# A fused attention and two-MLP kernel: every step that opens a PSUM bank takes the one of all eight that has been free longest

## The chip, the cores and the metric

One core of a Trainium2 chip. The metric is the device time of one execution in microseconds (us), lower is better. Before the change: 908.99 us, the median of 3 runs (908.58 to 909.68).

## The reference, cut to what matters

Linear attention over 4 batches of 8 heads with 576 tokens and 64 features, then two MLPs of 512 to 2048 to 512 on the 2304 tokens, with different activations; everything in float32.

```python
def phi(x):
    proj = np.einsum('bhsd,df->bhsf', x, w_phi)
    proj = proj - np.max(np.abs(proj), axis=-1, keepdims=True)
    return np.concatenate([np.exp(proj), np.exp(-proj)], axis=-1)
q_p, k_p = phi(q), phi(k)
kv = np.einsum('bhsf,bhsd->bhfd', k_p, v)
z = np.sum(k_p, axis=2)
num = np.einsum('bhsf,bhfd->bhsd', q_p, kv)
den = np.einsum('bhsf,bhf->bhs', q_p, z)[..., None] + 1e-06
x = num / den
...
h = x @ w_in                                   # MLP 1
x = np.where(h > 0.0, h, np.exp(np.minimum(h, 0.0)) - 1.0) @ w_out
...
h = x @ w_in                                   # MLP 2
x = (h * np.clip(h + 3.0, 0.0, 6.0) / 6.0) @ w_out
```

## The kernel before, in words

**Attention** runs in eight units (`unit`, L350) of one head pair and two batches. For a unit the steps are, with the names that the tables use:

- `PJ` (`proj`, L416): projections of k and q by `w_phi`, with 64 rows of the array each, in groups k0, k1, q0, q1 and x8 (the ninth block of both). A group opens two PSUM banks, one per head (h = 0, 1).
- `MX`, `SB` (`peak` L429, `shift` L437) on VectorE: the largest magnitude of a row, and the projection less it, out of PSUM into SBUF. The second of them frees the bank.
- `EX` on ScalarE (two exponentials), then `KV` (`kv`, L471): the sums over the tokens, 64 columns of the array wide, in two accumulator banks per unit; its x8 part uses 64 rows and 64 columns. `ST` on ScalarE copies the accumulators out.
- `QT` (`q_tr` L495, `q_tr8` L501): PE transposes of the shifted q, whole array; `QE` on ScalarE takes exponentials out of that bank.
- `NM` (`num`, L524): numerator and denominator, 64 columns wide, in three parts (ch = 0, 1, 2); `RT`, `RB` on VectorE divide; `XT` (`x_tr`, L552) transposes the quotient on PE, whole array; `XC` (`x_out`, L559) on ScalarE copies it to the MLP's input `x`.

**The MLPs** split a float32 value into two fp32r parts, form Strassen-like sums of blocks of x and w_in on VectorE, ScalarE and GpSimdE, and run 16 groups g of feature tiles each way: `hid` (L810, "P": six matmuls of 512 columns into an "h" bank), `hid4` (L824, "H": the block of the last 256 tokens), `join` (L842), the activation, `gate_lo` (L865, the last reader of an h bank, on VectorE), `outp` (L868, "O": the second matmul, into a "y" bank) and `sums` (L889, which adds the y bank to x and frees it). The first x blocks are used while the last attention unit still runs. The order of P, H and O on PE is written out in a list; PE's MLP steps follow it.

**What sets the order.** All of it is a list of `Step`s with engine, estimated duration, predecessors, and `Token`s that it takes from rings of buffers. `in_order` (L148) plays them against a model: per engine it takes, among the steps that could start within 0.3 us of the earliest, the one with the least rank. Ranks come from the tables `BIAS` (attention steps, by name, with other values in the first and last unit) and `SHIFT` (MLP steps), and `ON_POOL` names the steps that go to GpSimdE. `TURN` is the model's charge where PE goes from one shape of the array to another. The semaphores come from the data and buffers, so a step waits on the chip for whatever it needs, whenever that is.

**PSUM before.** The eight banks have fixed purposes. In attention four banks "p" take the projections in turn, two ("a0", "a1") the KV accumulators, two ("t") everything else (QT, NM, XT). In the MLPs the h steps take p0, p1, p2, p3, t1 in turn, the y steps a0, a1, t0 (`mlp_bank`, L711). A step that opens a bank waits for the readers of the one whose turn it is:

```python
BANKS = {"p": PB, "a0": 1, "a1": 1, "t": TB}
def bank(ring, shape=(128, 512)):
    i = count[ring] = count.get(ring, -1) + 1
    tag = ring if ring[-1].isdigit() else f"{ring}{i % BANKS[ring]}"
    return psum.tile(list(shape), F32, tag=tag, name="ps_" + tag)
...
HB, YB = ["p0", "p1", "p2", "p3", "t1"], ["a0", "a1", "t0"]
```

Of the kernel before, what the change touches and what calls it, by code (L numbers as in the profile page):

```python
# [8 lines left out]
F32 = mybir.dt.float32  # L9
# [13 lines left out]
PB, TB = 4, 2  # L23
# [94 lines left out]
}  # L118
ON_POOL = """
a01S20 a01S31 a10S10 a10S21 a10S30 a11S10 a11S11 l00S40 l00S41 l01A121 l01S41 l04x0 l04x1 l04x2  # L120
l10A220 l10S10 l10S21 l10S31 l11A110 l11S11 l11S41 l14x0 l14x1 l14x2
""".split()


# [23 lines left out]
def in_order(steps, rings):  # L148
# [30 lines left out]
    known = {}  # L179
# [1105 lines left out]
```

## Time and profile before

| | before |
|---|---|
| median of 3 runs | 908.99 us |
| the profiled execution's own time | 909.42 us |
| its span, first to last instruction | 907.6 us |
| PE (matmuls) busy | 894.1 us, 99% |
| VectorE busy | 662.1 us, 73% |
| ScalarE busy | 568.5 us, 63% |
| GpSimdE busy | 401.0 us, 44% |
| granted TensorE clock | 1.000 |
| matmul instructions in the trace | 6800 |

Attention takes the first 150 us or so, and the first MLP matmuls stand among its last ones; the first H step starts at 165.4 us; the second MLP begins near 526 us. After PE's last matmul some 3.9 us are left for the last sum and the last store. A float32 matmul outside the MLPs appears twice in the trace, so that 16 calls of `KV` are 32 matmuls of a row.

The busy share of PE counts each matmul from its start to a modelled end, and matmuls overlap. Idle time in a row stands behind the first instruction after it, with the instruction that is thought to have ended it.

### The profile page before, as it was taken

Reading aid. Unit: us, or ns where it says so; the run is one execution under the profiler, and the core shown is the slowest. Engines: PE = TensorE matmul, PEld = TensorE weight load, DVE = VectorE, ACT = ScalarE, POOL = GpSimd, SP = SyncE. Lnnn points to the kernel's source line nnn. Section 1 sums busy time; section 2 is a strip of 40 time slices with the busy share of each in tenths; the row PEclk is TensorE's granted clock in tenths of the full one; section 3 lists DMA queues with packets and bytes.
Section 4 is the critical chain, followed back from the end, with each engine's and each line's share of the span. In section 5 each row is a group of like instructions: output and inputs, shape, how many; then the busy total and the mean of one; then the engine's idle time right before and its main releaser. Section 6 shows DMA issues by size and latency. Waiting matters only on the chain.

```text
span 907.6 us, 17628 instructions
## 1 busy us (share of the span) xinstructions
PE 894.1 (99%) x6800; PEld 760.3 (84%) x6800; DVE 662.1 (73%) x1200; ACT 568.5 (63%) x1207; POOL 401.0 (44%) x574
## 2 busy tenths in 40 slices
PE   8999999999999999999999999999999999999998
PEld 7888888888888888888888878888888888888886
DVE  6888886856677676767677897577767666766655
ACT  6787777877665656666566777765545454546331
POOL 1447623244535353535343675665544444444200
PEclk9999999999999999999999999999999999999999
DMA  8544410001211111111111101112111111110013
GB/s 242 167 122 116 132 61 16 1 12 37 71 34 59 35 59 35 57 36 43 52 35 62 32 12 36 59 59 70 47 47 47 47 48 47 36 57 24 1 70 139
DMA packets 42675, 53.62 MB, mean 59 GB/s; under 512 B 21344, under 2 KB 21728, under 8 KB 42592
## 3 DMA queue, kind: packets, MB, share of 16 engines
q1 hardware_dynamic: 42448, 52.44, 18.7%
q8 instruction: 53, 0.87, 0.4%
q14 instruction: 30, 0.25, 0.1%
q10 hardware_dynamic: 144, 0.07, 0.0%
HBM read 47.78 MB, written 4.72 MB: 58 GB/s over the span
## 4 chain that ended last, share of the span: by engine, by line
PE 95%; DVE 2%; ACT 2%; issue 0%; DMA 0%; DVEq 0%
PE ps_a L884 29%; PE ps_p L818 27%; PE ps_t L884 14%; PE ps_t L818 6%; PE ps_t L534 4%; PE ps_p L422 4%; PE ps_a L484 4%; PE ps_p L832 3%; PE ps_t L498 2%; PE ps_t L832 1%; PE ps_t L556 1%; DVE mx L432 0%; ACT x L560 0%; ACT e L511 0%; DMA wphi<-in_w_phi_dram 0%
## 5 line engine op out<-in xcount | busy, mean ns | idle before, releaser
L818 PE MATMUL ps_p<-x_S,w_in 128*128 128x512 f32 x630 | 157.3, 390 | 0.0
L901 DVE TENSOR_TENSOR x<-ps_a,x 128x512 f32<-128x512 f32 (+1 forms) x178 | 116.6, 657 | 46.3 <-PE ps_a L884 44.1
L818 PEld LDWEIGHTS ps_p<-x_S,w_in 128*128 128x128 f32 x630 | 117.9, 188 | 24.4
L776 POOL TENSOR_TENSOR w_in<-w_bi,w_in 128x256 fp32r<-128x256 f32 x128 | 95.7, 766 | 73.9 <-ACT w_in L772 73.4
L818 PE MATMUL ps_p<-x_A,w_in 128*128 128x512 f32 x468 | 117.3, 390 | 1.4 <-DVE ga L866 1.4
L818 PEld LDWEIGHTS ps_p<-x_A,w_in 128*128 128x128 f32 x468 | 87.0, 188 | 19.2 <-DVE ga L866 1.6
L743 POOL TENSOR_SCALAR w_a<-w_a 128x256 f32<-128x256 f32 x128 | 53.5, 419 | 100.6 <-ACT w_a L738 97.1
L759 POOL TENSOR_TENSOR w_bi<-w_bi,w_a 128x256 int32<-128x256 int32 x64 | 49.2, 770 | 107.6 <-DVE w_a L755 107.6
L901 DVE TENSOR_TENSOR x<-ps_t,x 128x512 f32<-128x512 f32 (+1 forms) x89 | 59.0, 663 | 40.0 <-PE ps_t L884 39.0
L884 PE MATMUL ps_a<-w_out,gb 128*128 128x512 f32 (+1 forms) x342 | 82.7, 385 | 0.0
L884 PE MATMUL ps_a<-gb,w_out 128*128 128x512 f32 (+1 forms) x384 | 82.0, 355 | 0.6 <-DVE x L901 0.6
L785 POOL TENSOR_TENSOR w_out<-w_bo,w_out 128x256 fp32r<-128x256 f32 x64 | 48.0, 749 | 66.3 <-ACT w_out L781 65.6
L759 POOL TENSOR_TENSOR w_bo<-w_bo,w_a 128x256 int32<-128x256 int32 x64 | 48.6, 761 | 62.0 <-DVE w_a L755 62.0
L884 PEld LDWEIGHTS ps_a<-gb,w_out 128*128 128x128 f32 x384 | 65.2, 189 | 11.8 <-DVE x L901 0.8
L884 PEld LDWEIGHTS ps_a<-w_out,gb 128*128 128x128 f32 x342 | 63.5, 188 | 12.9
L884 PE MATMUL ps_a<-ga,w_out 128*128 128x512 f32 x258 | 64.0, 390 | 0.0
L859 DVE SCALAR_TENSOR_TENSOR ps_p<-ma,ps_p 128x512 f32<-128x512 f32 x66 | 45.8, 694 | 24.6 <-ACT ma L855 12.3
L884 PE MATMUL ps_a<-w_out,ga 128*128 128x512 f32 x240 | 58.5, 390 | 0.0
L840 ACT COPY mb<-ps_p 128x512 f32<-128x512 f32 x54 | 31.8, 588 | 41.4 <-PE ps_p L818 41.3
L432 DVE TENSOR_REDUCE mx<-ps_p 128x4 f32<-128x512 f32 (+1 forms) x80 | 49.7, 629 | 10.1 <-PE ps_p L422 10.1
L884 PEld LDWEIGHTS ps_a<-ga,w_out 128*128 128x128 f32 x258 | 47.8, 188 | 9.5
L738 ACT ACTIVATE w_a<-w 128x256 f32<-128x256 f32 x128 | 54.5, 426 | 0.5 <-POOL w_bi L759 0.3
(113 smaller groups left out, 1895.4 us busy)
## 6 DMA issues: line engine op xcount, KB each, us to landing
w<-in_moe_w_in_dram SPq DMA_DIRECT2D x64, 256.0 KB, 2.6
w<-in_moe_w_out_dram SPq DMA_DIRECT2D x64, 256.0 KB, 2.6
vb<-in_v_dram SPq DMA_DIRECT2D x16, 288.0 KB, 4.5
out_dram<-x SPq DMA_DIRECT2D x17, 256.0 KB, 2.0
raw_k<-in_k_dram SPq DMA_DIRECT2D x7, 576.0 KB, 4.7
raw_q<-in_q_dram SPq DMA_DIRECT2D x7, 576.0 KB, 4.0
raw_k<-in_k_dram SPq DMA_DIRECT2D x1, 320.0 KB, 4.1
raw_q<-in_q_dram SPq DMA_DIRECT2D x1, 320.0 KB, 4.5
```

The lines of the kernel that those rows point to most:

```text
L422: nc.tensor.matmul(out=ps[h][:, i * NF:(i + 1) * NF], lhsT=raw[s_][p, r * 128:(r + 1) * 128], rhs=wphi[p], start=True, stop=True,)
L432: V.tensor_reduce(out=mx[:, :n], in_=P[j, h], axis=AX.X, op=ALU.max, apply_absolute_value=True)
L484: nc.tensor.matmul(out=acc[bb][f0:f0 + 64, h, half], lhsT=kp[p, i, half, f0:f0 + 64], rhs=vb[u % 2][p, r, h], start=(done.count(bb) == 1 a ...
L738: nc.scalar.activation(out=st["a"], in_=s.bitcast(F32).rearrange("p (n t) -> p n t", t=2)[:, :, 1], func=AF.Abs)
L743: nc.gpsimd.tensor_scalar(out=st["a"], in0=st["a"], scalar1=W_MOST, scalar2=W_LEAST, op0=ALU.min, op1=ALU.max)
L759: nc.gpsimd.tensor_tensor(out=b_, in0=b_, in1=st["a"].bitcast(I32), op=ALU.add)
L776: nc.gpsimd.tensor_tensor(out=t[:, 1], in0=F[key], in1=t[:, 0].bitcast(F32), op=ALU.subtract)
L785: nc.gpsimd.tensor_tensor(out=t[:, 1], in0=F.pop((m, w, 1, c)), in1=t[:, 0].bitcast(F32), op=ALU.subtract)
L818: nc.tensor.matmul(out=PS[ps_], lhsT=t[:, a_, kk], rhs=X[pr, op][x_][kk], start=(opens and i == 0), stop=(i == 5), skip_group_check=True,)
L859: V.scalar_tensor_tensor(out=PS[ps_], in0=MAIN[key], scalar=s, in1=PS[ps_], op0=o0, op1=o1)
L884: nc.tensor.matmul(out=o, lhsT=a_, rhs=b_, start=(fi + j == 0), stop=(fi == 1 and j == 2), skip_group_check=half is not None,)
L901: V.tensor_tensor(out=part, in0=ps, in1=part, op=ALU.add)
```

## The change

`Token` gets a field `bank`. `in_order` keeps which token holds each of the eight banks; a step that opens a bank is possible once so many banks are free, and gets the one that has been free longest by the model. Rings still cap how many tokens of a kind are in use: p 6 instead of 4, t 4 instead of 2, a0 and a1 2 each instead of 1, h 5 and y 3 as before. So a projection group can open banks while five others are full, three groups in a row can be projected into six banks, and an h step can take a bank that last held a y tile. The four filling matmuls `WM` of the first unit now take a t token. The opening conditions "y" and "n" no longer wait for the users of the attention banks. `BIAS`, `SHIFT` and `ON_POOL` have new values throughout, so the order of the steps on all engines is new, in attention above all; the written list of P, H and O is the same.

```diff
-PB, TB = 4, 2
+PB, TB = 6, 4
...
-    "EX": 1217.6, "EXk00": -706.6, "EXk00@7": -744.6, "EXk01": 1256.6, "EXk01@0": 1292.5,
+    "EX": 813.1, "EXk00": -417.0, "EXk00@0": -376.4, "EXk00@7": -446.2, "EXk01": 875.0,
...
-        self.ring, self.users = ring, []
+        self.ring, self.users, self.bank = ring, [], None
...
+IN_BANKS = ("p", "a0", "a1", "t", "h", "y")
...
+    held = [None] * 8
+
+    def bank_free():
+        t = []
+        for k in held:
+            ends = [x.end for x in k.users] if k else []
+            t.append(None if None in ends else max([0.0] + [x.end + x.lag for x in k.users]) if k else 0.0)
+        return t
...
+        n = sum(k.ring in IN_BANKS for k in s.takes)
+        if n:
+            some = sorted(x for x in free_at if x is not None)
+            if len(some) < n:
+                return None
+            t = max(t, some[n - 1])
         return t
...
+            if k.ring in IN_BANKS:
+                t = bank_free()
+                k.bank = min((x, i) for i, x in enumerate(t) if x is not None)[1]
+                held[k.bank] = k
...
-    BANKS = {"p": PB, "a0": 1, "a1": 1, "t": TB}
-    rings = dict(BANKS)
-    count = {}
-
-    def bank(ring, shape=(128, 512)):
-        i = count[ring] = count.get(ring, -1) + 1
-        tag = ring if ring[-1].isdigit() else f"{ring}{i % BANKS[ring]}"
-        return psum.tile(list(shape), F32, tag=tag, name="ps_" + tag)
+    rings = {"p": PB, "a0": 2, "a1": 2, "t": TB}
+
+    def bank(i, kind, shape=(128, 512)):
+        return psum.tile(list(shape), F32, tag=f"b{i}", name=f"ps_{kind}{i}")
...
-            ps = [bank("p") for _ in range(2)]
+            ps = [bank(Tk["p", j, h].bank, "p") for h in range(2)]
...
-                add("WM", "PE", FILL * 0.218, fill, behind=[S_[pj]])
+                Tk["wm"] = take("t")
+                add("WM", "PE", FILL * 0.218, fill, behind=[S_[pj]], takes=[Tk["wm"]], uses=[Tk["wm"]])
...
-        "y": step("NONE", 0.0, y_open, after=y_users, rank=BEGIN),
-        "n": step("NONE", 0.0, y_open, after=n_users, rank=BEGIN),
+        "y": step("NONE", 0.0, y_open, rank=BEGIN),
+        "n": step("NONE", 0.0, y_open, rank=BEGIN),
...
-    def mlp_bank(ring):
-        i = nxt[ring] = nxt.get(ring, -1) + 1
-        tag = (HB if ring == "h" else YB)[i % rings[ring]]
-        return psum.tile([128, 512], F32, tag=tag, name="ps_" + tag)
-
...
-            PS[ps_] = mlp_bank("h")
+            PS[ps_] = bank(ptok[ps_].bank, "h")
```

Three places in the new order. In the rows a PSUM tile is named by its bank before the change (p0 to p3, a0, a1, t0, t1) and by its kind and bank number after it (p, a, t, n, h, y with 0 to 7); the number behind it counts tiles.

**Place 1: PE, where one attention unit passes into the next.** Before, one of six equal passages: XT, the transpose of x8, two NM parts, the next unit's first two KV steps, XT.

```order
L556 MATMUL ps_t1_2284<-ident_66,nr_2273 128x128 x3
L504 MATMUL ps_t0_2290<-ident_66,sh8_1879 128x128 x2
L534 MATMUL ps_t1_2302<-st_2182,e_2172 64x65 x4
...
L534 MATMUL ps_t0_2334<-st_2182,e_2232 64x65 x4
...
L484 MATMUL ps_a0_2369<-vb0_105,kp_2331 64x65 x16
L484 MATMUL ps_a1_2370<-vb0_105,kp_2364 64x65 x16
L556 MATMUL ps_t1_2420<-ident_66,nr_2367 128x128 x3
```

With the change, a passage between two units:

```order
L518 MATMUL ps_t0_2116<-ident_66,shq_1702 128x128 x4
L524 MATMUL ps_t4_2126<-ident_66,sh8_1357 128x128 x2
L518 MATMUL ps_t3_2133<-ident_66,shq_1933 128x128 x4
L518 MATMUL ps_t6_2140<-ident_66,shq_1886 128x128 x4
L554 MATMUL ps_n1_2153<-st_1754,e_1849 64x65 x4
...
L554 MATMUL ps_n0_2189<-st_1754,e_2130 64x65 x4
...
L504 MATMUL ps_a4_2229<-vb0_105,kp_2181 64x65 x16
```

Before, the first NM opens t1, which the XT two rows above it filled; now the transposes stand together, in four different banks, and the NM parts open two others.

**Place 2: PE, second MLP, first feature group.** The last terms of the first pair of token blocks (P3 and P4), H, and the first two terms of the second pair. Before:

```order
L818 MATMUL ps_p2_6771<-x_S4_0_2948,w_in_6689 128x512 x6
L818 MATMUL ps_t1_6853<-x_A22_0_114,w_in_6820 128x512 x6
L832 MATMUL ps_p1_6885<-x_b4_2949,w_in_6687 128x256 x6
L832 MATMUL ps_p1_6885<-x_b4_2949,w_in_6689 128x256 x6
L818 MATMUL ps_p2_6950<-x_A11_1_3135,w_in_6654 128x512 x6
L818 MATMUL ps_p3_6963<-x_A12_1_3136,w_in_6672 128x512 x6
```

With the change:

```order
L833 MATMUL ps_h3_6770<-x_S4_0_2830,w_in_6692 128x512 x6
L833 MATMUL ps_h6_6852<-x_A22_0_114,w_in_6756 128x512 x6
L847 MATMUL ps_h7_6878<-x_b4_2831,w_in_6690 128x256 x6
L847 MATMUL ps_h7_6878<-x_b4_2831,w_in_6692 128x256 x6
L833 MATMUL ps_h0_6944<-x_A11_1_3141,w_in_6654 128x512 x6
L833 MATMUL ps_h2_6956<-x_A12_1_3142,w_in_6656 128x512 x6
```

The order is the same; the last two steps open banks 0 and 2, which held y tiles of the first MLP, instead of p2, which P3 filled four rows above, and p3.

**Place 3: PE, the end of attention, up to the first H.** Before:

```order
L534 MATMUL ps_t0_3063<-st_2897,e_3004 64x65 x4
L818 MATMUL ps_p0_2952<-x_S4_0_2948,w_in_828 128x512 x6
L818 MATMUL ps_p2_2984<-x_A22_0_114,w_in_968 128x512 x6
L556 MATMUL ps_t1_3115<-ident_66,nr_3060 128x128 x3
L556 MATMUL ps_t0_3122<-ident_66,nr_3103 128x128 x3
L832 MATMUL ps_t1_3146<-x_b4_2949,w_in_398 128x256 x6
```

With the change:

```order
L833 MATMUL ps_h1_2832<-x_S4_0_2830,w_in_903 128x512 x6
L833 MATMUL ps_h2_2931<-x_A22_0_114,w_in_987 128x512 x6
L576 MATMUL ps_t0_3035<-ident_66,nr_3022 128x128 x3
L518 MATMUL ps_t5_3040<-ident_66,shq_2811 128x128 x4
L524 MATMUL ps_t4_3046<-ident_66,sh8_2518 128x128 x2
L554 MATMUL ps_n3_3057<-st_2808,e_2898 64x65 x4
...
L554 MATMUL ps_n7_3087<-st_2808,e_2926 64x65 x4
L576 MATMUL ps_t0_3119<-ident_66,nr_3115 128x128 x3
L576 MATMUL ps_t5_3130<-ident_66,nr_3126 128x128 x3
L847 MATMUL ps_h4_3151<-x_b4_2831,w_in_625 128x256 x6
```

Before, two MLP terms stand between the last NM and the last two XT; now those terms come first, and the last QT, both NM parts and the last two XT follow one another directly.

## Rows read from the trace of the kernel before

**Rows 1.** The page: span and PE's busy time.

```profile
span 907.6 us, 17628 instructions
PE 894.1 (99%) x6800; PEld 760.3 (84%) x6800; DVE 662.1 (73%) x1200; ACT 568.5 (63%) x1207; POOL 401.0 (44%) x574
```

**Rows 2.** Stretches: length, then busy us (instructions) per engine, clock, DMA share, GB/s.

```profile
62.39:80.44 18.05, 17.70 (x403) 15.90 (x404) 16.18 (x34) 14.99 (x37) 11.18 (x14) 1.00 0.48 133
165.37:520.00 354.63, 354.63 (x1731) 300.50 (x1732) 255.78 (x458) 239.46 (x495) 165.19 (x238) 1.00 0.13 42
520.00:550.00 30.00, 27.95 (x144) 23.61 (x143) 28.71 (x43) 21.10 (x43) 21.02 (x21) 1.00 0.03 9
```

**Rows 3.** PE's waits, whole span: waiting line, releaser, us in total, times, longest.

```profile
PE ps_t L534 <- ACT x L560: 2.1, 6, 0.4
PE ps_p L818 <- DVE ga L866: 1.4, 1, 1.4
PE ps_p L422 <- PE ps_a L404: 0.9, 1, 0.9
PE ps_a L484 <- issue: 0.9, 1, 0.9
PE ps_t L534 <- ACT e L511: 0.7, 1, 0.7
PE ps_a L884 <- DVE x L901: 0.6, 1, 0.6
PE ps_t L534 <- ACT st L493: 0.5, 1, 0.5
PE ps_t L832 <- ACT x L560: 0.2, 1, 0.2
PE ps_p L422 <- DVE shk L446: 0.2, 1, 0.2
```

**Rows 4.** ScalarE's timeline: the copy of a quotient, and a pair of exponentials.

```profile
61.86 0.48 ACT L560 COPY x<-ps_t 128x384 f32<-128x384 f32 x1 [0.77 <-PE ps_t L556]
77.45 1.09 ACT L511 ACTIVATE e<-ps_t 128x512 f32<-128x512 f32 x2
```

**Rows 5.** The chain of waits in one attention unit: start, us, what.

```profile
62.39 3.02 PE ps_t L534 x96
65.41 1.87 PE ps_a L484 x64
70.36 1.08 PE ps_a L484 x32
71.92 0.44 PE ps_t L498 x4
73.44 0.59 PE ps_t L498 x4
74.03 0.65 PE ps_p L422 x8
75.26 1.56 PE ps_t L534 x48
77.41 1.98 PE ps_p L422 x32
```

**Rows 6.** PE's timeline: two steps that waited.

```profile
9.32 1.16 PE L422 MATMUL ps_p<-wphi,raw_k 64*128 64x128 f32 x16 [0.95 <-PE ps_a L404]
544.25 3.02 PE L818 MATMUL ps_p<-x_A,w_in 128*128 128x512 f32 x12 [1.43 <-DVE ga L866]
```

**Rows 7.** VectorE's timeline: two last readers of a bank, and the division of one NM part.

```profile
8.54 0.68 DVE L446 TENSOR_TENSOR shk<-ps_p,mx 128x512 f32<-128x512 f32 x1
65.46 0.17 DVE L542 TENSOR_SCALAR dn<-ps_t 128x6 f32<-128x6 f32 x1 [0.42 <-PE ps_t L534]
65.88 0.56 DVE L547 TENSOR_TENSOR nr<-ps_t,dn 128x384 f32<-128x384 f32 x1
543.50 0.69 DVE L866 TENSOR_TENSOR ga<-ps_p,ga 128x512 fp32r<-128x512 f32 x1
```

More of the change, by code (lines that the diff above doesn't have):

```diff
@@ L65 @@
 SHIFT = {
[52 rows of a table removed]
[53 rows of a table added]
 }
 ON_POOL = """
-a01S20 a01S31 a10S10 a10S21 a10S30 a11S10 a11S11 l00S40 l00S41 l01A121 l01S41 l04x0 l04x1 l04x2
-l10A220 l10S10 l10S21 l10S31 l11A110 l11S11 l11S41 l14x0 l14x1 l14x2
+a01S11 a01S41 a10S10 a10S21 a10S30 a11S10 a11S20 a11S40 l00S40 l00S41 l01S10 l01S21 l01S40 l04x0
+l04x2 l10A220 l10S10 l10S21 l11A121 l11A220 l11S21 l11S31 l14x1 l14x3
 """.split()
@@ L176, in soonest @@
                 t = max(t, x.end + x.lag)
+        n = sum(k.ring in IN_BANKS for k in s.takes)
[4 more added lines that the diff above has]
+            t = max(t, some[n - 1])
         return t
-    known = {}
     while len(out) < len(steps):
         best = None
+        free_at = bank_free()
         for e, some in ready.items():
@@ L328, in attention_then_two_mlps @@
     wphi = apool.tile([128, NF], F32, name="wphi")
-    warm = bank("t")
+    warm = bank(7, "w")
     for _ in range(WARM):
@@ L401, in fill @@
         def fill():
-            ps = bank("a1")
+            ps = bank(Tk["wm"].bank, "w")
             for _ in range(FILL):
@@ L474, in kv @@
                 for bb in range(2):
-                    acc[bb] = bank(f"a{bb}", (128, 2, 2, D + 1))
+                    acc[bb] = bank(Tk["acc", bb].bank, "a", (128, 2, 2, D + 1))
             rs = [r for s_, r in ITEMS[j] if s_ == "k"]
@@ L495, in q_tr @@
         def q_tr(h, c):
-            ps = bank("t")
+            ps = bank(Tk["q", h, c].bank, "t")
             for i in range(4):
@@ L501, in q_tr8 @@
         def q_tr8():
-            ps = bank("t")
+            ps = bank(Tk["q", 8].bank, "t")
             for h in range(2):
@@ L524, in num @@
         def num(ch):
-            ps = bank("t", (128, 3, 2, D + 1))
+            ps = bank(Tk["n", ch].bank, "n", (128, 3, 2, D + 1))
             for i in range(3):
@@ L552, in x_tr @@
         def x_tr(ch):
-            ps = bank("t")
+            ps = bank(Tk["x", ch].bank, "t")
             nr = NR.pop(ch).rearrange("p i h d -> p i (h d)")
@@ L571, in unit @@
             tp = {(j, h): take("p") for j in js for h in range(2)}
+            Tk.update({("p",) + x: t for x, t in tp.items()})
             need = sorted({x for s_, r in items for x in ld[s_, int(r >= 4)]})
@@ L616, in unit @@
                 t, te = take("t"), take("e")
-                Tk["e", h, c] = te
+                Tk["e", h, c], Tk["q", h, c] = te, t
                 add(f"QT{h}{c}", "PE", 4 * 0.109, bind_(q_tr, h, c), after=[f"SBq{c}{h}"], takes=[t],
@@ L621, in unit @@
                     uses=[t], stage="QE")
-        t = take("t")
+        t = Tk["q", 8] = take("t")
         add("QT8", "PE", 2 * 0.109, q_tr8, after=["SBx80", "SBx81"], takes=[t], uses=[Tk["sh8"]], stage="QT")
@@ L628, in unit @@
             t, td, tn, tx = take("t"), take("dn"), take("nr"), take("t")
+            Tk["n", ch], Tk["x", ch] = t, tx
             cs = [[0], [0, 1], [1]][ch]
@@ L702, in attention_then_two_mlps @@
         "b": step("NONE", 0.0, open_b, after=b_users, rank=BEGIN),
-        "y": step("NONE", 0.0, y_open, after=y_users, rank=BEGIN),
-        "n": step("NONE", 0.0, y_open, after=n_users, rank=BEGIN),
-    }
-    HB, YB = ["p0", "p1", "p2", "p3", "t1"], ["a0", "a1", "t0"]
-    rings.update({"s": 2, "ca": 2, "bi": 4, "bo": 2, "wi": 8, "wo": 3, "h": len(HB), "y": len(YB),
+        "y": step("NONE", 0.0, y_open, rank=BEGIN),
+        "n": step("NONE", 0.0, y_open, rank=BEGIN),
+    }
+    rings.update({"s": 2, "ca": 2, "bi": 4, "bo": 2, "wi": 8, "wo": 3, "h": 5, "y": 3,
                   "ma": 2, "mb": 2, "ga": 2, "gb": 2})
-    nxt = {}
-    def mlp_bank(ring):
-        i = nxt[ring] = nxt.get(ring, -1) + 1
-        tag = (HB if ring == "h" else YB)[i % rings[ring]]
-        return psum.tile([128, 512], F32, tag=tag, name="ps_" + tag)
     F, WI, WO = {}, {}, {}
@@ L825, in hid4 @@
         if fi == 0:
-            PS[ps_] = mlp_bank("h")
+            PS[ps_] = bank(ptok[ps_].bank, "h")
         i = 0
@@ L843, in join @@
         if to != ps_:
-            PS[to] = mlp_bank("h")
+            PS[to] = bank(ptok[to].bank, "h")
         V.tensor_tensor(out=PS[to], in0=PS[ps_], in1=MAIN[key], op=ALU.add)
@@ L866, in gate_lo, with outp @@
         V.tensor_tensor(out=GG[key][:, 1], in0=PS.pop(ps_), in1=GG[key][:, 0].bitcast(F32), op=ALU.subtract)
-    def outp(m, g, b, d, half=None):
+    def outp(m, g, b, d, ty, half=None):
         n = BLOCKS[b][1]
-        ps = Y[b, d] = mlp_bank("y") if not half else Y[b, d]
+        ps = Y[b, d] = bank(ty.bank, "y") if not half else Y[b, d]
         cols = slice(0, 512) if half is None else slice(256 * half, 256 * half + 256)
@@ L1182, in attention_then_two_mlps @@
                 for half in range(2):
-                    s = step("PE", us / 2, bind_(outp, m, g, b, d, half), rank=clock, behind=[tail], uses=[ty],
+                    s = step("PE", us / 2, bind_(outp, m, g, b, d, ty, half), rank=clock, behind=[tail], uses=[ty],
                              takes=[] if half else [ty], after=[tiles[g, b, 0], tiles[g, b, 1], OUT[g, 0], OUT[g, 1]])
@@ L1190, in attention_then_two_mlps @@
             fis = (0,) if b == 4 else (0, 1)
-            s = step("PE", us, bind_(outp, m, g, b, d), rank=clock, behind=behind, takes=[ty],
+            s = step("PE", us, bind_(outp, m, g, b, d, ty), rank=clock, behind=behind, takes=[ty],
                      after=[tiles[g, b, fi] for fi in fis] + [OUT[g, 0], OUT[g, 1], OPEN["y"], OPEN["n"]],
```

173 rows, old and new, of tables (BIAS, SHIFT) are left out of this document.

## The prediction, made before the changed kernel ran

> **What bounds the kernel now.** I read the page first, then the table of stretches, then PE's list of waits, then single waits in the timelines. The page has PE busy for 894.1 of 907.6 us [rows 1], so nothing but PE's own time and its 13.5 us of idle can be won. The stretches show where that idle lies. From 165 to 520 us PE has no idle at all, 354.63 of 354.63 us, while VectorE has 255.78 [rows 2]: the MLPs are PE's, and a new order on the other engines is hidden there. Two places differ. An attention unit has 18.05 us with PE at 17.70 and VectorE at 16.18, and the passage from the first MLP to the second (520 to 550 us) has PE at 27.95 of 30.00 with VectorE at 28.71 [rows 2]. The granted clock is 1.00 in all of them, the upper of its two levels.
>
> The list of waits names what PE stood idle for [rows 3]. I sort it by what the step lacked: a bank, or its data.
>
> - Six times 0.35 us, 2.1 in all, NM waits for ScalarE's copy of a quotient. That is a bank: place 1 has XT, x8's transpose and NM in t1, t0, t1. The copy of such an XT begins at 61.86 and takes 0.48 us, so it ends at 62.34 [rows 4], and NM starts at 62.39 [rows 5].
> - 0.95 us before the first unit's second k projection at 9.32 [rows 6]. The row names the filling matmuls, which had ended by then. The p banks go round four, so this group needs those of k0; the shift that frees one of them runs from 8.54 for 0.68 us, to 9.22 [rows 7]. A bank, unless the load of k1 landed then too.
> - 1.43 us at 544.25, in the second MLP [rows 6]. Place 2: the step opens p2, which P3 had filled. Its last reader, the gate's low part, runs from 543.50 for 0.69 us, to 544.19 [rows 7]. A bank.
> - 0.6 us of an O step for a sum (three y banks, four O steps in a row), 0.2 us of the first H for a copy (its t1 held an XT), 0.2 us of x8's projection for a shift [rows 3]. Banks too.
>
> Together 2.1 + 0.95 + 1.43 + 0.6 + 0.2 + 0.2 = 5.5 us. Data waits are 0.9 ("issue"), 0.7 (exponentials) and 0.5 us (the statistics copy) [rows 3], 2.1 us, and the change doesn't address them.
>
> **A second cost lies inside PE's busy time.** When PE goes from one shape of the array to another, the next step takes longer. A QT behind an XT, both whole array, takes 0.44 us, behind a KV 0.59: 0.15 us for the turn. A projection of 8 takes 0.65 and one of 32 takes 1.98, so (1.98 - 0.65) / 24 = 0.055 each, 8 of them 0.44, and the turn 0.21. NM of 96 takes 3.02 and of 48 takes 1.56, so 48 cost 1.46 and the turn 0.10; KV takes 1.08 alone and 1.87 / 2 = 0.94 behind NM, which gives 0.14 [rows 5]. The busy row says otherwise: by it only idle can go, and the unit has 18.05 - 17.70 = 0.35 us of it [rows 2].
>
> The Trainium skill (Perfetto Trace Analysis, Identifying the Most-Contended Engine) holds that matmul occupancy is a poor measure of how near a kernel is to its limit, since pipelined matmuls hide time in it. By the busy row alone the turns below would be worth nothing and the sum would come to 905.5 us; by the rule such time may be there. The chain's rows side with the rule, with 0.10 to 0.21 us a turn, and I go by them.
>
> **The change, part by part.**
>
> *Fewer turns.* I counted the turns on PE up to the first H in both orders: 115 before, 100 now. Into the whole array 48 become 31, into projections 24 become 21, into KV and NM 35 become 38, into x8's KV 8 become 10. So -17 x 0.15 = -2.55, -3 x 0.21 = -0.63, +3 x 0.12 (between 0.10 and 0.14) = +0.36, and +2 x 0.15, for which no row stands alone (between the 0.10 and 0.21 of its neighbours, nearest to the middle) = +0.30. Sum -2.5 us; with all fifteen at 0.10 or 0.21 it is -1.5 to -3.15. Place 1 shows how they go: four transposes in a row where there were XT and one, and NM next to NM and KV.
>
> *Bank waits.* At place 1 the NM parts open banks other than those of the transposes just before. At place 2 the first term of the second pair opens bank 0, last a y tile; by the written list P6, P7, P5, H, P3, P4 and H stand between, seven steps of about 1.4 us (two take 3.02 with their turn [rows 6]), so that sum is long done. What is late next there is the O step behind P1 and P2, which wants the gate's low part that ended at 544.19; P1 and P2 take 2.7 us, so it comes at 545.5 and finds it done. The first unit's k0, q0 and k1 now take six banks. I count all of it: -5.5 us. Bounds: 0 (each wait meets its data a moment later) and -5.5.
>
> *Waits that the new order makes.* Place 3: the last XT now stands right behind the last NM. VectorE's division starts 0.05 us after NM's end (65.46 against 62.39 + 3.02) and ends at 65.88 + 0.56 = 66.44, 1.03 us after it [rows 5, 7]; only an XT of 0.48 lies between, so +0.55 us, where two MLP terms covered it before. Elsewhere I take a wait of the present size, 0.35, at four of the passages: +1.4. Together +2.0. Bounds: 0, and 8 (one pair of exponentials, 1.09 us [rows 4], waited for in seven or eight units).
>
> *The rest.* GpSimdE's and VectorE's steps change places and a few change engines; in the MLPs PE's full stretches cover them [rows 2]. If that cover went, each late VectorE step would cost its 0.68 us. In attention VectorE would have 16.18 us in a unit of about 17.4, still under PE. The load queue keeps its contents, at a DMA share of 0.48 [rows 2]: nothing. The opening conditions y and n only let model steps start.
>
> *Sum*, against the profiled execution's 909.42 us: 909.42 - 2.5 - 5.5 + 2.0 = 903.4. That execution is 0.43 above the median, so **903.0 us**.
>
> **The rivals.**
>
> 1. *No waits left at all.* The data waits (2.1) go too and none is made: 909.0 - 2.5 - 5.5 - 2.1 = 898.9. For it: the order was made anew with more freedom. Against it: place 3, and exponentials and statistics come no sooner.
> 2. *The waits only move.* The projections may now hold six of eight banks until VectorE has read them, and QT and NM find none free. Waits as large as those removed, only the turns are won: 906.5. For it: VectorE has 90% of a unit. Against it: at places 1 and 2 no opened bank belongs to a recent step. The Trainium skill speaks for this rival (TensorEngine Tiling (Array Packing), Restrictions and Gotchas): row tiling raises the pressure on PSUM, as row tiles write to different banks; the projections here do, two banks a group.
> 3. *The change doesn't do what it says.* "Free longest" holds in the model; on the chip readers run in another order, and the banks chosen are the late ones; what the turns save is spent on these waits: 909.0.
> 4. *Slower: ScalarE at the passages.* At place 1 three QT and x8's transpose stand together, 0.59 + 0.2 + 2 x 0.44 = 1.67 us of PE, and give ScalarE three pairs of 1.09, the last done at 0.59 + 3.27 = 3.86. If the NM right behind needs the last pair, it waits 3.86 - 1.67 - 0.1 = 2.1 us, at six passages 12.6: 909.0 - 8.0 + 12.6 + 0.55 = 914.1. It decides from 1.3 us a passage. Against it: the first NM there begins with e_1849, exponentials older than these transposes.
>
> **How the numbers follow.** Forecast 0.53, rival 1 0.12, rival 2 0.16, rival 3 0.08, rival 4 0.11. A difference of 0.2% (1.8 us) is about what a measurement of this kernel can tell from no change, so faster means under 907.2. The forecast, rival 1 and most of rival 2 (0.13) make faster, less 0.01 for the forecast's own upper end: 0.77. Rival 3, what is left of rivals 2 and the forecast, and the mildest of rival 4 (0.01) make the same 0.13; the rest of rival 4 slower, 0.10. The range goes from the largest gain, 909.0 - 3.15 - 5.5 - 2.1 = 898.2, to 908.3, which takes in rival 2 and half of rival 3; left out are rival 4, the other half of rival 3 and some 0.03 below.
>
> **What the profile afterwards would show.** The turns: a first H some 3 to 6 us earlier than 165.4. The bank waits: no wait of NM for the quotient's copy, the k1 projection directly behind q0, PE without idle from 520 to 550 us. The new wait: the last XT idle for about 0.5 us behind VectorE. Rival 2 would show projections or QT waiting for VectorE's shifts; rival 4 NM waiting for exponentials, several times over 1 us. I am wrong if PE's waits before the first H add up to more than 7 us, or if a step of the same shape behind a turn takes no longer than without one.

## The result and the profile after

| | before | after |
|---|---|---|
| median | 908.99 us (5 runs, 908.33 to 910.26) | 899.58 us (5 runs, 899.25 to 900.19) |
| ratio to before | | 0.9896, 95% interval 0.9881 to 0.9910 |
| the profiled execution, its span | 909.42, 907.6 us | 900.16, 898.1 us |
| granted clock | 1.000 | 1.000 |

The change is worth 9.4 us. 903.0 was forecast; the time lies inside the range, nearer to rival 1 (898.9).

The page of after, span and busy time, against [rows 1]:

```profile
span 898.1 us, 17626 instructions
PE 891.3 (99%) x6800; PEld 761.1 (85%) x6800; DVE 651.5 (73%) x1200; ACT 566.1 (63%) x1207; POOL 400.4 (45%) x574
```

PE lost 6.7 us of idle (13.5 to 6.8) and 2.8 us of busy time, for the same 6800 matmuls. PE's list of waits after, against [rows 3]:

```profile
PE ps_w L352 <- DVE blank L326: 1.1, 1, 1.1
PE ps_p L442 <- DMA wphi<-in_w_phi_dram: 0.5, 1, 0.5
PE ps_t L576 <- DVE dn L562: 0.4, 1, 0.4
PE ps_t L576 <- DVE nr L567: 0.4, 1, 0.4
PE ps_t L576 <- ACT e L531: 0.3, 1, 0.3
PE ps_t L524 <- DVE shq L466: 0.3, 1, 0.3
PE ps_n L554 <- ACT e L531: 0.2, 1, 0.2
```

The first two are the start of the program, in both kernels. Every bank wait of [rows 3] is gone, and so are the three data waits that were expected to stay. What is new is at the bottom: five waits of 0.2 to 0.4 us, 1.51 in all. Two are for banks again, by what they wait for: an XT at 73.40 (0.28 us) for exponentials, and x8's transpose at 85.54 (0.28 us) for a shift of q. Neither reads these, so it must be their bank that it opens. Two are the last two XT, at place 3 (PE's timeline of after):

```profile
7.43 1.06 PE L442 MATMUL ps_p<-wphi,raw_k 64*128 64x128 f32 x16
...
157.46 0.52 PE L576 MATMUL ps_t<-ident,nr 128*128 128x128 f32 x3 [0.43 <-DVE dn L562]
158.34 0.52 PE L576 MATMUL ps_t<-ident,nr 128*128 128x128 f32 x3 [0.37 <-DVE nr L567]
158.62 3.65 PE L847 MATMUL ps_h<-x_b,w_in 128*128 128x256 f32 x24
...
535.17 2.91 PE L833 MATMUL ps_h<-x_A,w_in 128*128 128x512 f32 x12
```

The first row is the k1 projection, which began at 9.32 after 0.95 us of idle [rows 6] and now follows its forerunner at once; the last is place 2, which had 1.43 us. The stretch around it has no idle now, against 27.95 of 30.00 in [rows 2]:

```profile
512.00:542.00 30.00, 30.00 (x157) 25.76 (x155) 27.96 (x44) 21.97 (x46) 22.79 (x23) 1.00 0.00 1
```

Where the time went is read best from the starts of the same PE step in two traces. H occurs all through the MLPs (its rows in the timelines; "banks alone" is the first experiment below):

| H step | before | banks alone | after | before less after |
|---|---|---|---|---|
| second of the first MLP | 191.78 | 188.00 | 185.41 | 6.37 |
| last of the first MLP | 515.25 | 511.47 | 508.88 | 6.37 |
| first of the second MLP | 537.05 | 533.14 | 529.56 | 7.49 |
| third of the second MLP | 567.51 | 561.90 | 558.32 | 9.19 |

From there to the last matmul the distance stays 9.19, and 0.3 us come from the last store. So 6.37 us were won in attention, nothing in the full stretch of the first MLP, 1.12 and 1.70 us at the two waits of the passage. Up to the second H of the first MLP PE's idle fell from 7.59 to 3.24 us, both with the start; the other 2.02 of the 6.37 came out of PE's busy time.

### The profile page after: what moved, and what is told of

Read it like the earlier page. It is cut to its first block, busy times and chain, and to the rows that moved or that the text cites. A ratio compares the mean times of both kernels' runs of the same rounds, so it can differ in the third digit from the quotient of the medians.

```text
span 898.1 us, 17626 instructions
## 1 busy us (share of the span) xinstructions
PE 891.3 (99%) x6800; PEld 761.1 (85%) x6800; DVE 651.5 (73%) x1200; ACT 566.1 (63%) x1207; POOL 400.4 (45%) x574
## 4 chain that ended last, share of the span: by engine, by line
PE 97%; DVE 2%; ACT 1%; DMA 0%; issue 0%; DVEq 0%; ACTq 0%
PE ps_y L899 44%; PE ps_h L833 34%; PE ps_h L847 5%; PE ps_p L442 4%; PE ps_a L504 4%; PE ps_n L554 4%; PE ps_t L518 2%; PE ps_t L576 1%; DVE mx L452 0%; DVE shq L466 0%; DMA wphi<-in_w_phi_dram 0%; ACT e L531 0%; DVE nr L567 0%; PE ps_t L524 0%; DVE shk L466 0%
## 5 line engine op out<-in xcount | busy, mean ns | idle before, releaser
L916 DVE TENSOR_TENSOR x<-ps_y,x 128x512 f32<-128x512 f32 (+1 forms) x267 | 175.0, 659 | 86.1 <-PE ps_y L899 83.4
L833 PE MATMUL ps_h<-x_S,w_in 128*128 128x512 f32 x768 | 189.8, 389 | 0.0
L833 PEld LDWEIGHTS ps_h<-x_S,w_in 128*128 128x128 f32 x768 | 143.9, 188 | 29.8
L833 PE MATMUL ps_h<-x_A,w_in 128*128 128x512 f32 x576 | 143.8, 390 | 0.0
L833 PEld LDWEIGHTS ps_h<-x_A,w_in 128*128 128x128 f32 x576 | 107.2, 188 | 21.6
L899 PE MATMUL ps_y<-gb,w_out 128*128 128x512 f32 (+1 forms) x576 | 118.8, 354 | 0.0
L899 PE MATMUL ps_y<-w_out,gb 128*128 128x512 f32 (+1 forms) x486 | 117.5, 386 | 0.0
L899 PEld LDWEIGHTS ps_y<-gb,w_out 128*128 128x128 f32 x576 | 97.0, 189 | 16.1
L899 PEld LDWEIGHTS ps_y<-w_out,gb 128*128 128x128 f32 x486 | 90.6, 188 | 18.5
L899 PE MATMUL ps_y<-ga,w_out 128*128 128x512 f32 x384 | 92.6, 390 | 0.0
L899 PE MATMUL ps_y<-w_out,ga 128*128 128x512 f32 x384 | 92.3, 390 | 0.0
```

Of the source, the lines that this page charges most:

```text
L833: nc.tensor.matmul(out=PS[ps_], lhsT=t[:, a_, kk], rhs=X[pr, op][x_][kk], start=(opens and i == 0), stop=(i == 5), skip_group_check=True,)
L899: nc.tensor.matmul(out=o, lhsT=a_, rhs=b_, start=(fi + j == 0), stop=(fi == 1 and j == 2), skip_group_check=half is not None,)
L916: V.tensor_tensor(out=part, in0=ps, in1=part, op=ALU.add)
```

## The experiments

Three theories. **T**: the free choice of banks removes PE's bank waits, and the new order removes turns of the array. **R1**: the new ranks alone do it. **R2**: the choice of banks alone does it. In each diff "..." stands for what is left out.

### The banks alone

The tables, caps and opening conditions of before; every engine's instructions stand in the order of before, and only the bank differs.

```diff
+            if k.ring in IN_BANKS:
+                t = bank_free()
+                k.bank = min((x, i) for i, x in enumerate(t) if x is not None)[1]
+                held[k.bank] = k
...
-            ps = [bank("p") for _ in range(2)]
+            ps = [bank(Tk["p", j, h].bank, "p") for h in range(2)]
```

> The tables, the caps and with them the order of every instruction on every engine are those of before (115 turns of the array up to the first H); only the physical bank is the one of eight that the model has free longest. Theory T (bank waits cost PE some 5.5 us as idle and up to 1.6 us more hidden in its busy time, and the new order wins about 2 us by turns): 902.0 to 904.0 us, no wait of NM for the quotient's copy, no 1.43 us at the second MLP's first group, the first H at about 161. Rival R1 (it is the new order of the tables, the choice of banks is nothing): 909.0, the six waits of 0.35 us stay as waits for something else. Rival R2 (the choice of banks is all of it): 899.6.

Measured: 903.81 us, ratio 0.9941 (0.9927 to 0.9954): 5.1 us of the 9.4. PE's waits:

```profile
PE ps_t L506 <- DVE shq L454: 0.8, 2, 0.5
PE ps_n L542 <- ACT st L501: 0.5, 1, 0.5
PE ps_h L821 <- POOL w_in L779: 0.4, 1, 0.4
PE ps_a L492 <- ACT kp L463: 0.4, 2, 0.2
PE ps_n L542 <- ACT e L519: 0.2, 1, 0.2
```

No wait for a quotient's copy is left, and none at place 2. R1 and R2 both fall: the banks give a good half. Three bank waits were not won but replaced. In the first unit the 0.95 us at k1 went, but two QT now wait for VectorE's shifts (0.8 together), and the first NM comes only 0.15 us sooner (23.99, now 23.84). The first H no longer waits for a copy, but its second half now waits for the block that VectorE makes, and the half microsecond that its start had gained is lost again. At the passage the O step no longer waits for a sum, but a term two steps on waits for weights that GpSimdE rounds:

```profile
528.32 2.00 PE L821 MATMUL ps_h<-x_S,w_in 128*128 128x512 f32 x8
530.75 2.56 PE L821 MATMUL ps_h<-x_S,w_in 128*128 128x512 f32 x10 [0.43 <-POOL w_in L779]
```

Of the 1.12 us there, 0.13 were won; the other 0.99 come with the new tables only, under which no term waits for weights there. The 0.87 us that before showed as "issue" is gone, though nothing moved; it is not in the next run either.

### The banks of the MLPs alone

As above, but the attention tiles keep the fixed banks of before.

```diff
+                fixed = {"p": i % 4, "a0": 4, "a1": 5, "t": 6 + (i + 1) % 2, "w": 5}
+                k.bank = fixed[k.ring] if k.ring in fixed else min((x, i) for i, x in enumerate(t) if x is not None)[1]
```

> Order of before on all engines; only the h and y tiles of the MLPs choose among eight banks, attention keeps its fixed ones. T: of the 9.4 us won, the traces put 1.12 at the O step that stood idle for 0.60 and 1.70 at the term that stood idle for 1.43, so 909.0 - 2.8 = 906.2 us, with the first H still at 165.4 and then the distance to before growing to 2.8. If only the idle shown is worth anything: 909.0 - 2.0 = 907.0. R1: 909.0.

Measured: 907.03 us, ratio 0.9979 (0.9970 to 0.9987), 1.9 us. The six waits of 0.35 us stand again in the list ("PE ps_n L544 <- ACT x L570: 2.1, 6, 0.4"), place 2 has none, and the same 0.43 us for the weights is there. 2.8 was expected; what is missing is that wait: by the starts of H the passage gives 0.12 and 1.70 us. This trace leads that of before by another 1.4 us in attention, where banks and order are those of before: 0.65 in the first 9 us and 0.8 at the "issue" row. Two single traces can differ by that much, and it is not the banks' doing.

### The new tables with the caps of before, fixed banks and free banks

Two kernels with the same order on every engine, caps p 4 and t 2: the first is the kernel before with the new tables, the second the changed kernel with one line altered.

```diff
-    "EX": 1217.6, "EXk00": -706.6, "EXk00@7": -744.6, "EXk01": 1256.6, "EXk01@0": 1292.5,
...
+    "EX": 813.1, "EXk00": -417.0, "EXk00@0": -376.4, "EXk00@7": -446.2, "EXk01": 875.0,
...
```

```diff
-PB, TB = 6, 4
+PB, TB = 4, 2
```

> The new tables with the fixed banks and the caps of before (p 4, a 1 and 1, t 2). The order is new, but not that of the change, since the caps bind: 126 turns up to the first H where before has 115 and the change 100. R1 (the tables win it): about 900. T: the bank waits are back, and 11 turns of 0.10 to 0.21 us more: not faster than before, 909 to 913 us, with waits of NM, XT or QT for ScalarE's or VectorE's readers of the bank.

> The same order as the run with the new tables and fixed banks, instruction for instruction on every engine, but each step that opens a bank gets the one of eight free longest; the caps stay at p 4 and t 2. T: the bank waits go, the 126 turns stay (26 more than the change has, 2.6 to 5.5 us): 902 to 905.5 us, 4 to 9 below the run with fixed banks. Rival (caps are what matters, banks nothing): within 1 us of the run with fixed banks. Rival (turns cost nothing): 899.6, as the change.

Measured: 927.10 us with fixed banks, ratio 1.0201 (1.0187 to 1.0215); 922.80 with free ones, 1.0154 (1.0140 to 1.0168). Free banks win 4.3 us under this order too. But both are far slower than before, which no theory had said. The largest waits of the second, and of the first:

```profile
PE ps_h L847 <- DVE x_b L819: 10.1, 1, 10.1
PE ps_h L833 <- ACT mb L855: 1.8, 2, 1.1
```

```profile
PE ps_t L837 <- DVE x_b L809: 10.1, 1, 10.1
PE ps_t L561 <- DVE nr L552: 1.9, 3, 0.7
PE ps_t L539 <- ACT e L516: 1.9, 7, 0.6
PE ps_t L539 <- DVE nr L552: 1.6, 2, 0.8
```

One H waits 10.1 us for a block that VectorE makes; the bank waits of the first kernel (NM and XT behind readers) are gone in the second. Ranks that were found for one set of caps do not fit another.

### The old tables with the planner and caps of the change

```diff
-PB, TB = 6, 4
...
-    "EX": 813.1, "EXk00": -417.0, "EXk00@0": -376.4, "EXk00@7": -446.2, "EXk01": 875.0,
...
+    "EX": 1217.6, "EXk00": -706.6, "EXk00@7": -744.6, "EXk01": 1256.6, "EXk01@0": 1292.5,
...
+PB, TB = 6, 4
```

> The planner of the change (eight banks, caps 6, 4, 2, 2) with the tables of ranks of before: 97 turns up to the first H, where before has 115 and the change 100. T (banks 5.1 us as the run with the banks alone showed, and turns of 0.10 to 0.21 us each): 909.0 - 5.1 - 18 x 0.15 = 901.2, between 900 and 903, new tables or not, with the wait for the weights' rounding at the second MLP perhaps still there. Rival (without tables searched for it the room only makes new waits): 904 and more, with waits on VectorE or ScalarE that add up to more than 3 us in attention.

Measured: 914.68 us, ratio 1.0067 (1.0053 to 1.0080). The time is the rival's (904 or more), but both T and the rival had the place wrong: in attention the waits do not grow by 3 us, and the first H starts at 160.32, 0.8 us before that of the banks alone (161.10). Then one O step stops:

```profile
170.64 1.52 PE L894 MATMUL ps_y<-ga,w_out 128*128 128x512 f32 x6
180.89 2.93 PE L894 MATMUL ps_y<-gb,w_out 128*128 128x512 f32 x6 [8.73 <-ACT gb L873]
183.62 2.16 PE L828 MATMUL ps_h<-x_S,w_in 128*128 128x512 f32 x6
```

So free banks and caps are no gain in themselves: they let PE run ahead, and the ranks have to bring VectorE's and ScalarE's work for the first feature group in time.

### The price of a turn

Stretches of matmuls on zeros ahead of the program: two shapes once in blocks and once in eight alternations.

```diff
+    for a, na, b, nb in ((whole, 4, rows64, 8), (whole, 4, cols64, 16), (rows64, 8, cols64, 16)):
+        a(8 * na)
+        b(8 * nb)
+        for _ in range(8):
+            a(na)
+            b(nb)
```

> The changed kernel with stretches of matmuls on a tile of zeros put ahead of everything: for each pair of shapes (whole array and 64 rows; whole array and 64 columns; 64 rows and 64 columns) the same matmuls once in two blocks and once in eight alternations, 14 turns more. T, by the prices of 0.15 (into the whole array), 0.21 (into 64 rows) and 0.12 (into 64 columns): the alternating stretch is longer than the two blocks by 2.5 us, 1.9 us and 2.3 us. Rival (turns cost nothing, and the longer steps behind them in the trace are due to something else): under 0.3 us each.

Measured, from the starts: alternating 17.44 us against 14.68 in blocks (whole array and 64 rows), 17.36 against 14.96, 17.38 (seven of its eight pairs took 15.21) against 14.97: 2.8, 2.4 and 2.4 us for 14 turns (the first whole-array block runs on from whole-array matmuls, without a turn; the second pair's stands for it). Solved for the three shapes, 0.20 into the whole array, 0.20 into 64 rows, 0.15 into 64 columns. Turns cost, and the rival falls. But these whole-array steps were matmuls, and the kernel's are transposes; the next run takes those.

> As the run with the price of turns, but the whole-array steps are transposes (four a step, as QT has), with a control: two steps of the same 64-column shape into different banks, alternating. Then six times a step of whole-array matmuls that waits for VectorE to copy the step before it. T, by the first such run (0.20 into the whole array, 0.20 into 64 rows, 0.15 into 64 columns): 14 turns add 2.7 us for transposes and 64 rows, 2.4 us for transposes and 64 columns, 2.4 us again for 64 rows and 64 columns, and nothing for the control. Rival, by the kernel's own rows (0.15 into a transpose, and 15 turns fewer gave 2.3 us): 0.3 to 0.8 us less where transposes stand, 2.0 and 1.8 us. The waits: if the idle that the trace shows before a matmul is all that is lost, starts of equal steps lie apart by their own length and that idle; if more is lost, as at the O step (0.60 shown, 1.12 lost) and at the term of the second MLP (1.43 shown, 1.70 lost), by 0.3 to 0.5 us more.

The timeline: "L364" is the transposes, "L370" 64 rows, "L375" 64 columns.

```profile
14.79 3.66 PE L364 MATMUL ps_w<-ident,blank 128*128 128x128 f32 x32
18.37 7.42 PE L370 MATMUL ps_w<-blank 64*128 64x128 f32 x128
25.72 0.66 PE L364 MATMUL ps_w<-ident,blank 128*128 128x128 f32 x4
26.30 1.16 PE L370 MATMUL ps_w<-blank 64*128 64x128 f32 x16
...
39.14 3.71 PE L364 MATMUL ps_w<-ident,blank 128*128 128x128 f32 x32
42.78 7.69 PE L375 MATMUL ps_w<-blank 128*64 128x65 f32 x256
50.40 0.66 PE L364 MATMUL ps_w<-ident,blank 128*128 128x128 f32 x4
50.99 1.15 PE L375 MATMUL ps_w<-blank 128*64 128x65 f32 x32
...
63.75 7.42 PE L370 MATMUL ps_w<-blank 64*128 64x128 f32 x128
```

In blocks, transposes and 64 rows take 25.72 - 14.79 = 10.93 us with one turn; alternating, 39.14 - 25.72 = 13.42 with sixteen: 2.49 for 15 turns. Transposes and 64 columns: 50.40 - 39.14 = 11.26 against 63.75 - 50.40 = 13.35, 2.09 for 14. The third pair gives 2.41 again. Solved: **0.145 us into transposes, 0.19 into 64 rows, 0.155 into 64 columns**. The control adds nothing: 1056 matmuls of the 64-column shape, half of them alternating between two banks, take 30.94 us, 0.029 each, as the block's 7.62 / 256 does. It is the shape that costs, not the bank.

In the kernels themselves the trace has the start of every matmul. Take for each turn how much later than at the usual spacing of their shape the next matmuls (up to four) start. The middle value for a pair of shapes agrees within 0.01 us between the kernel with the banks alone and the change: 0.14 from the whole array into 64 columns and 0.18 back, 0.19 into 64 rows and 0.20 back, 0.22 from 64 columns into 64 rows and 0.20 back, up to 0.24 out of x8's KV. That is a little more than in the blocks above.

The second half of that run asks what a wait costs beyond its idle:

```profile
128.41 2.05 PE L393 MATMUL ps_w<-blank,b 128*128 128x128 f32 x16 [0.38 <-DVE b L390]
130.30 1.95 PE L359 MATMUL ps_w<-blank 128*128 128x128 f32 x16
132.63 2.05 PE L393 MATMUL ps_w<-blank,b 128*128 128x128 f32 x16 [0.38 <-DVE b L390]
```

From 128.41 to 132.63 are 4.22 us. Without a wait or a turn these matmuls start 0.112 us apart, so that sixteen take 1.79 and two steps 3.57: the wait costs 0.65, 0.27 more than the 0.38 shown. Some 0.16 of that is the last matmul ahead of the wait, drawn 0.275 long where the next could have started after 0.112; 0.10 is the first one behind it, whose successor starts 0.214 after it. 0.3 to 0.5 was expected.

### Without the filling matmuls

```diff
-    WARM, FILL = 5, 4
+    WARM, FILL = 5, 0
```

> The changed kernel without the four filling matmuls on zeros at 8.41 us (they compute nothing that is used), every other instruction in the same order on every engine. They hold PE 1.09 us, from 8.41 to 9.50. If PE's own time bounds the first unit: 898.5 us. T by the trace: the transpose at 10.59 needs the shift that ends at 9.92, so PE wins 0.67 us there at most, and VectorE, busy without a gap from 6.11 us on, does not come sooner, so the next units of work wait for it: 899.0 to 899.6 us, with new waits of QT and KV for VectorE and ScalarE before 22 us.

Measured: 900.19 us, ratio 0.9906 (0.9892 to 0.9919), no different from the change. QT now waits 1.1 us in two places for VectorE's shifts; the 1.09 us of filling lay in time that PE had to spend anyway. So in the change's first unit VectorE is the bound, not PE.

### Filling the end of attention

The two new waits at place 3 invite a version better than both: put the last MLP term before the first H behind the last NM. The second and third kernels also raise the rank of activations that came late in the first.

```diff
+        if x == ("P", 0, 0, "P4"):
+            behind = behind + [NM[NU - 1, 2]]
```

```diff
-    "g0.0": 142.7, "g0.1": 80.1, "g0.2": -54.5, "g0.4": 19.7, "g1.0": -2.6, "g1.1": 7.0,
+    "g0.0": 0.0, "g0.1": 80.1, "g0.2": -54.5, "g0.4": 19.7, "g1.0": -2.6, "g1.1": 7.0,
```

(the third: g0.1 at 0.0 too)

> The changed kernel with one edge more: the last MLP term before the first H, which stands ahead of the last XT steps' numerators, is put behind the last NM, so that 1.4 us of PE's work lies between that NM and the last two XT, as before the change. They stood idle for 0.43 and 0.37 us. T: those two waits go, 899.6 - 0.8 = 898.8 us. If an idle gap costs more than is shown, as the two in the second MLP did: down to 898.3. Rival: NM of the last part then waits for the exponentials instead, or the activation of the first feature group comes later: 899.6 or more.

> The kernel that fills the end of attention, with one rank changed: the activation steps of the first feature group's first block come 142.7 us less late in the ranking (SHIFT g0.0 from 142.7 to 0), so that on VectorE and ScalarE they stand ahead of steps that prepare the later blocks, nearly as in the change. T (in the run before this PE won 0.95 us at the end of attention and lost 8.1 us behind it, to one wait of 4.75 us for a gate tile and the lower clock that followed, because VectorE's order had changed): no wait over 1 us behind the first H and 898.3 to 899.2 us. Rival (the moved term itself comes too late for the gate, whatever the order on VectorE): the wait stays, at 3 us or more, and the time over 904.

> As the run beside it, but the activation steps of the second block of the first pair come 80.1 us less late too (SHIFT g0.1 from 80.1 to 0): they now stand ahead of the block that H multiplies. T: O no longer waits for a gate, but H may wait for its block, since VectorE makes it 35 steps of order later; 898.3 to 899.2 if that wait stays under 1 us, 900 to 905 if not. Rival (the term itself comes too late): a wait of O of 3 us or more and over 904.

Measured: 906.82 us (ratio 0.9976, 0.9967 to 0.9985), 905.72 (0.9962, 0.9950 to 0.9975) and 915.80 (1.0076, 1.0062 to 1.0090), all slower than the change. PE's timeline of the first:

```profile
154.97 1.67 PE L834 MATMUL ps_h<-x_A,w_in 128*128 128x512 f32 x6
156.48 0.82 PE L576 MATMUL ps_t<-ident,nr 128*128 128x128 f32 x6
157.05 3.70 PE L848 MATMUL ps_h<-x_b,w_in 128*128 128x256 f32 x24
160.59 0.86 PE L900 MATMUL ps_y<-ga,w_out 128*128 128x512 f32 x3
166.20 6.75 PE L900 MATMUL ps_y<-ga,w_out 128*128 128x512 f32 x15 [4.75 <-ACT ga L879]
```

The edge does what it should: the XT wait no more, and from the XT of unit 7's first part (152.49 in the change, 150.50 here) to H lie 6.55 us with the term among them, where the change needs 6.13 and the term's 1.37: 0.95 us won. Then O stops for a gate. In the second kernel it stops for the other gate (4.17 us, gb), in the third H stops for its block:

```profile
174.26 3.20 PE L848 MATMUL ps_h<-x_b,w_in 128*128 128x256 f32 x14 [11.68 <-DVE x_b L820]
```

ahead of which it had also waited 3.58 us for ScalarE's part of that block.

VectorE and ScalarE make all that was late. ScalarE casts the gate tile `ga` that O waits for ahead of the six x_A blocks in the change (first rows), and behind them and three x_S blocks in the first kernel, where O starts when this cast ends:

```profile
156.77 0.57 ACT L878 CAST ga<-ps_h 128x512 fp32r<-128x512 f32 x1
...
159.72 3.22 ACT L816 CAST x_A<-x 128x512 fp32r<-128x512 f32 x6
```

```profile
158.21 3.22 ACT L817 CAST x_A<-x 128x512 fp32r<-128x512 f32 x6
...
163.72 1.94 ACT L817 CAST x_S<-x 128x512 fp32r<-128x512 f32 x3
165.57 0.58 ACT L879 CAST ga<-ps_h 128x512 fp32r<-128x512 f32 x1
```

They had not fallen behind in work: up to 158 us VectorE has been busy for 129.69 us in both kernels, ScalarE for 119.69 in this one and 120.34 in the change. It is the order of their work: in the second kernel, with the rank raised, this cast comes at 155.36 and O runs on from 160.51, and the wait is for a `gb` instead, with the time over 904 and the wait over 3 us that the rival there had named. The clock behind the wait, in stretches of the first kernel:

```profile
166.00:170.00 4.00, 3.75 (x8) 2.55 (x9) 3.91 (x6) 2.54 (x5) 4.00 (x3) 0.50 0.00 0
170.00:174.00 4.00, 4.00 (x14) 3.12 (x14) 2.92 (x5) 2.21 (x4) 0.29 (x1) 0.71 0.00 0
174.00:178.00 4.00, 4.00 (x19) 3.33 (x18) 2.16 (x4) 3.14 (x7) 2.44 (x3) 1.00 0.00 0
```

Whether an order exists in which none of these steps is late stays open.

## Why the prediction was right, and which terms were off

**The chances and the sign** rested on two mechanisms, both confirmed: the waits sorted as bank waits were bank waits (under an unmoved order, free banks remove them), and turns lie inside PE's busy time.

**Turns: -2.5 forecast, -2.3 found.** From the banks alone to the change the second H moves 2.59 us, PE's idle before it falls by 0.29 (3.53 to 3.24), so 2.30 came from busy time, with fifteen turns fewer, 0.15 each. By the prices per pair of shapes the turns up to the first H cost 20.81 us with the banks alone and 18.51 in the change: 2.30 again. No run takes turns away and leaves all else, and busy time holds more than turns: with 97 turns the old tables' run has 156.15 us of it ahead of the first H, 0.7 more than the change with 100, for the same 3284 matmuls. By the prices of the transposes' run the same counts give -17 x 0.145 - 3 x 0.19 + 3 x 0.155 = -2.57, and with 0.155 for the two turns into x8's KV, whose shape was not run, -2.26. The prices taken from the chain (0.15, 0.21, 0.12) were good to 0.04, and PE's busy row, by which none of this could be won, fell by 2.8 us, 2.0 in attention and 0.8 at the passage. The Trainium skill (TensorEngine Tiling (Array Packing), Key Properties) says that a change of the tiling mode drains the engine. The runs agree that each turn costs time, 0.145 to 0.19 us in the blocks; that a drain is the reason no run shows.

**Bank waits: the total right, partly by luck, the parts not.** 5.1 us were measured for the 5.5 forecast, but from the starts of the same matmuls in the traces of before and of the banks alone, the waits that were sorted as banks gave about 4.5: six copies 0.42 each, k1 0.15, the first H nothing, the O step 0.13, the term 1.70. The rest is the exponentials' wait, sorted as data, and in this trace the "issue" row. The 0.95 us of k1 were not won by the banks, since VectorE's shifts were late next; the prediction asked that at place 2 but not here. The waits in the second MLP were worth more than their idle: 1.12 for 0.60 and 1.70 for 1.43. The term's 0.27 on top is what a shown wait of 0.38 cost on top in the run above. For the O step part of it is a wait that the list does not hold. In before, the O step's first twelve matmuls of 256 columns took 1.71 us to the next start; in the change 24 take 2.87, so twelve 1.43: some 0.27 us of waiting are drawn as busy. The Trainium skill (Perfetto Trace Analysis, Optimization Strategy) holds that the same gap, repeating on the engine that should be full, can mean too little room for the next tile; the six equal gaps of 0.35 us were that, and went with free banks.

**The step that failed: data waits that the change leaves, and the waits that the new order makes, +2.0.** The sum kept 2.1 us of data waits and added 2.0. In the change all three data waits are gone: 0.87 ("issue") also in the two runs of the unmoved order, so it belonged to no step that the change touched, and its cause stays open; the exponentials' 0.74 is 0.15 with the banks alone and 0.74 with the MLPs' alone, so free attention banks do bring exponentials sooner, which the prediction denied; the statistics' 0.5 stays in both and goes with the new order only. New waits came to 1.5 us, of which 0.8 at the last two XT (0.55 was forecast there) and 0.7 elsewhere (1.4 forecast). That is 2.6 us too pessimistic. Another 0.8 us is the passage, which gave 2.82 where the rows showed 2.03. Against the spans that closes: 4.35 of idle in attention, 2.02 of PE's busy time, 2.82 at the passage and 0.3 at the store are 9.5, as 907.6 - 898.1.

**The rivals.** Rival 1 gave nearly the time, but not for its reason: waits were made, and others paid for them. Rival 2 (only the turns won) and rival 3 fall with the banks alone. What rival 2 would show is there once, x8's transpose behind a shift for 0.28 us. Rival 4's place shows nothing: the transposes stand together at the passages, and the only NM that waits for exponentials does so for 0.2 us. Of what the profile was to show, the first H came a little earlier than said (6.75 us, not 3 to 6), and the rest as said. One reading was wrong without weight: the 3.02 us of two MLP terms hold no turn, since the H ahead of them is whole array too; they stand behind a wait.

**What was not foreseen** is that the parts do not add. Free banks with the old tables at the old caps give 5.1 us, the new tables at the old caps lose 13.9, the old tables at the new caps lose 5.9 (against 908.95 and 908.82 us, the medians of before beside them), and the whole wins 9.4. Both losses are in the main one wait of 8.7 to 10.1 us in the first feature group, with the lower clock behind it.

## What to carry to other kernels

Before giving a wait a price, ask what the waiting step lacked, a buffer or its data, and for a buffer wait look up when the data comes: a buffer that is free sooner wins only up to that moment (0.15 of 0.95 us at k1). Count the changes of array shape on the matmul engine; they stand in no list of waits, and at 0.14 to 0.24 us each the hundred that are left are 18.5 us, 2% of this kernel. And treat ranks, caps and the rule for buffers as one: a table searched for one set moved 13.9 us the wrong way under another, mostly through one late step on an engine that was not the bound.

## What the runs showed of the hardware

The granted clock fell behind long waits, and the slower matmuls came on top of the wait. In the first kernel that fills the end, PE stood idle for 4.75 us up to 166.20; the clock was 0.50 from 166 to 170 us, the lower level of 1.2 GHz, 0.71 on average from 170 to 174, and 1.00 again after that (rows above). Its fifteen matmuls took 172.79 - 166.20 = 6.59 us, where the change's eighteen take 166.22 - 162.11 = 4.11, 3.43 for fifteen: 3.2 us on top of 4.75. Behind the 8.73 us of the old tables' run six matmuls took 183.62 - 180.89 = 2.73 us and the next six 2.00, where 1.36 is usual: 2.0 us on top. The waits of up to 1.43 us in the kernel before left the clock at 1.00 [rows 2], and the longest cost 0.27 on top (1.70).
